# Attention beside a gated feed-forward block on one core: exponent chains of three score pairs on VectorE, merged output groups, and another rule for when paired score tiles are issued

## The chip, the cores and the metric

The kernel runs on one core of one Trainium2 chip. The time is device microseconds of one execution; of several executions the median is given. A separate execution is profiled, and every instruction time below comes from that one.

## What is computed

The input has 2048 rows of 512 bf16 numbers. It is layer-normalized, and the result goes into two branches whose outputs are added to the input: attention with 32 heads of 16 columns, and a gated feed-forward block of width 1792.

```python
def _A_ref(x, wqkv, wo):                     # H = 32, Dh = 16
    qkv = (x @ wqkv).reshape(B, S, 3, H, Dh).transpose(2, 0, 3, 1, 4)
    q, k, v = qkv[0], qkv[1], qkv[2]
    scores = einsum("bhqd,bhkd->bhqk", q, k) * (Dh ** -0.5)
    o = einsum("bhqk,bhkd->bhqd", softmax(scores, axis=-1), v)
    return o.transpose(0, 2, 1, 3).reshape(B, S, D) @ wo

def _B_ref(x, w1, w3, w2):                   # F = 1792
    return (silu(x @ w1) * (x @ w3)) @ w2

return x + _A_ref(layernorm(x), ...) + _B_ref(layernorm(x), ...)
```

The attention needs 32 x 2048 x 2048 exponentials, which is most of the work outside TensorE.

## The kernel before

**Planning.** The program is written by a planner, `_plan_fast`. It steps through time in 0.02 us, keeps a modelled free time for each engine (`P.free`), and whenever an engine is free it picks the next operation for it. The outcome is a fixed order of instructions for each engine, with semaphore waits where data or buffers need them. The planner's durations only decide this order; on the chip an instruction starts when its engine reaches it and its semaphores allow it. A second program, `_plan_max`, stands behind a check of the value ranges; it is in the instruction lists but doesn't run with these inputs.

**Units, pairs and PSUM.** Queries are taken in four chunks of 512 and heads in eight groups of four, which makes 32 units. Inside a unit a score pair is two heads by 128 keys by 512 queries: two matmuls into two neighbouring PSUM banks (`score`, the matmuls at L1803), 128x1024 numbers in all. There are 1056 pairs; the last unit is split into two halves of 256 queries. Banks 0 to 5 are three pair buffers (`pbuf`), bank 6 is the tenant of all dense tiles (projections, feed-forward, output), and bank 7 collects the value products of a unit.

**Two ways to an exponent.** A pair goes to ScalarE (`try_a`, `one_a`): one activation with Exp over 1024 columns (L1866), from PSUM into one of 12 `PT` slots. Or it goes to VectorE (`try_d`): the instruction `p1` (L1939) adds a constant to the scaled score, clips it and writes int16, so that the bits read as a bf16 number near the exponential. Then `chain` improves it with four VectorE instructions on SBUF, over all pairs of a slot at once: `m` (L1981) takes mantissa bits, `g` (L1997) gives a second term, `t` (L1988, two inputs) multiplies, and `e` (L2003) keeps the exponent bits in place. The sum of `e`, `t` and `g` stands for the exponential, so a VectorE pair has three operands where a ScalarE pair has one, and the value matmuls (`try_pv`, L2066) take all three. The slots are three `y`, two `m` and two `g` slots in the tile `xd`, each two pairs (2048 columns) wide; `xd` also holds the input at the start. A chain covers two pairs, except near the end.

**The rule of due times.** `open_bufs` lists the pair buffers that are free. `try_d` issues a score for VectorE if `d_due` allows it: VectorE must be free within `D_SOON` = 0.6 us (`D_RIDE` = 1.0 if a score has just been issued, since matmuls on other rows of the array can run beside it), and the previous chain must have come far enough. `hold_d` lets one such score be outstanding at a time. `try_a` issues one or two scores for ScalarE. With one free buffer it may wait, until `A_SOON` = 0.7 us before ScalarE's queue is modelled to run dry, if a second buffer will be free by then (`A_OVER` = 0.1 more); two pairs with different rows of the array are then issued together. In this test a buffer that is in use and whose release isn't planned yet counts as never free.

**Dense tiles and outputs.** K, Q and V tiles are taken from `crit` a fixed number of score rows before they are needed. Feed-forward and output tiles come from the list `bg`, as filler between scores. A feed-forward tile (`tiles_FFN`) is two dense tiles: G, followed by a tanh on ScalarE (L1555) and a product on VectorE (L1559), and Y, whose product (L1569) writes one of the 14 slots of `hT`. An output tile (`tile_OUT`, 128 rows) is made in two parts: part 3 adds up the 14 feed-forward groups and is evicted with the input added into a float32 sum `osum` (L1619); part 4 adds up the 8 attention groups, later, and is evicted with `osum` added (L1630). The next chunk's feed-forward waits until part 3 has read all of `hT` (`HF`). The last chunk uses parts 3 and 2, and part 5 for the last tile.

**The end of a unit.** `unit_end` copies the value products to SBUF (L2086), and DMAs gather and spread the row sums, VectorE takes the reciprocal (L2106), and GpSimd normalizes (L2127). GpSimd works only beside `p1` (`beside_p1`). The last two halves (`last_end`) use TensorE for the row sums and the spreading (L2168, L2187), VectorE for reciprocal and normalization (L2174, L2195), and ScalarE for the very last copy (L2160).

## Time and profile before

| | |
|---|---|
| median of 3 runs | 790.03 us (788.83 to 790.27) |
| the profiled execution | 789.84 us |
| its span, first to last instruction | 788.1 us |
| ScalarE exponents (L1866) | 796, mean 1151 ns |
| VectorE first steps (L1939) | 228, mean 1216 ns |
| granted TensorE clock, mean | 0.997 |

"Span" runs from the first to the last instruction; some 1.7 us lie around it. Busy time is the union of what an engine's instructions last. Two neighbours on ScalarE or VectorE overlap at their edges[...], so the mean of a group is longer than the pace at which the engine takes such instructions; the pace is the distance between two starts in the timeline. A matmul that stands in the page as 32x512 uses a quarter of the array; four of them on different quarters run side by side and are called a group here. A shape such as 128x2048 is partitions by columns.

The granted clock stays at full speed in nearly all slices, and the DMA engines are busy for about a quarter of the time. POOL is busy for 12% of the span.

### The profile page before, as it was taken

To read this page: it belongs to the slowest core of one execution; us is meant where nothing else is said; L and a number is where in the kernel's file an instruction comes from. 1 tells how busy PE (TensorE), PEld (TensorE's weight loads), DVE (VectorE), ACT (ScalarE), POOL (GpSimd) and SP (SyncE) were. 2 spreads that over 40 slices of the span, in tenths; PEclk is the share of its full clock that TensorE was granted. 3 is DMA by queue.
4 is the path that set the end of the run, shared out by engine and by line. 5 is a ranking of instruction groups with operands and counts; after the bars stand their busy time and mean duration, and the time that the engine had idled before them with its cause. 6 is when DMAs were issued, how large, how long until landed. Compare 5 with 4: busy or idle time off the path is not lost.

```text
span 788.1 us, 21640 instructions
## 1 busy us (share of the span) xinstructions
PE 747.1 (95%) x9337; PEld 226.8 (29%) x9337; DVE 764.8 (97%) x1023; ACT 768.5 (98%) x870; POOL 90.7 (12%) x120
## 2 busy tenths in 40 slices
PE   8999999999999999999999999999899999999997
PEld 6422222222222222222222222222222222222234
DVE  8899999999999999999999999999999999999995
ACT  6999999999999999999999999999999999999994
POOL 3200021002020010201102020010201103010000
PEclk9999999999999999999999999999999999999999
DMA  7023122322332222333302234322222332232121
GB/s 215 2 22 115 9 36 30 49 21 40 51 43 22 30 41 38 47 49 45 50 14 34 22 55 56 41 35 38 34 29 23 56 43 39 49 52 16 20 25 33
DMA packets 83441, 32.94 MB, mean 42 GB/s; under 512 B 72072, under 2 KB 79496, under 8 KB 83336
## 3 DMA queue, kind: packets, MB, share of 16 engines
q1 hardware_dynamic: 83336, 31.46, 28.0%
q8 instruction: 75, 1.23, 0.6%
q14 instruction: 30, 0.25, 0.1%
HBM read 22.81 MB, written 2.10 MB: 32 GB/s over the span
## 4 chain that ended last, share of the span: by engine, by line
ACT 82%; PE 11%; DVE 5%; issue 0%; DMA 0%; POOL 0%; DVEq 0%; ACTq 0%
ACT f_PT L1866 78%; PE ps L1332 4%; PE ps L1803 4%; ACT f_th L1555 3%; PE ps L2066 3%; DVE f_xd L1939 1%; DVE f_xd L1988 1%; DVE f_xd L2003 0%; DVE f_xd L1981 0%; DMA f_xd<-in_A_x_dram 0%; DVE f_hT L1569 0%; PE ps L1344 0%; DVE f_t L1559 0%; DVE f_stats L1256 0%; DVE f_xd L1997 0%
## 5 line engine op out<-in xcount | busy, mean ns | idle before, releaser
L1866 ACT ACTIVATE f_PT<-ps 128x1024 bf16<-128x1024 f32 x796 | 744.7, 1151 | 3.4 <-PE ps L1803 3.2
L1803 PE MATMUL ps<-f_QT,f_KT 32*128 32x512 bf16 (+1 forms) x2112 | 313.6, 378 | 23.3 <-ACT f_PT L1866 17.2
L1939 DVE TENSOR_SCALAR f_xd<-ps 128x1024 int16<-128x1024 f32 x228 | 277.2, 1216 | 2.8 <-PE ps L1803 2.5
L2066 PE MATMUL ps<-f_PT,f_Vaug 128*17 128x512 bf16 (+2 forms) x1640 | 205.1, 378 | 1.1 <-DVE f_U L2086 0.5
L2066 PE MATMUL ps<-f_xd,f_Vaug 128*32 128x512 bf16 (+2 forms) x1416 | 181.9, 377 | 4.6 <-DVE f_U L2086 3.1
L1803 PEld LDWEIGHTS ps<-f_QT,f_KT 32*128 32x128 bf16 x2112 | 80.5, 91 | 322.0 <-ACT f_PT L1866 262.1
L1332 PE MATMUL ps<-f_xnT,f_w 128*32 128x512 bf16 x1792 | 143.1, 386 | 3.7 <-DVE f_t L1559 1.6
L1988 DVE TENSOR_TENSOR f_xd<-f_xd 128x2048 bf16<-128x2048 bf16 (+1 forms) x115 | 139.7, 1215 | 0.0
L1471 POOL TENSOR_SCALAR f_QT<-f_QT,f_msk 128x256 bf16<-128x256 bf16 x60 | 55.3, 922 | 270.5 <-DVE f_xd L1997 112.8
L1981 DVE TENSOR_SCALAR f_xd<-f_xd 128x2048 int16<-128x2048 int16 (+1 forms) x115 | 78.1, 679 | 3.9 <-PE ps L2066 3.1
L2003 DVE TENSOR_SCALAR f_xd<-f_xd 128x2048 int16<-128x2048 int16 (+1 forms) x115 | 78.3, 681 | 0.0
L1997 DVE TENSOR_SCALAR f_xd<-f_xd 128x2048 int16<-128x2048 int16 (+1 forms) x115 | 78.2, 680 | 0.0
L1332 PE MATMUL ps<-f_w,f_hT 128*32 128x512 bf16 x896 | 73.2, 383 | 0.2 <-DVE f_xn_sb L1630 0.2
L2127 POOL TENSOR_TENSOR f_onorm<-f_U,f_R 128x256 bf16<-128x256 f32 x30 | 25.4, 854 | 375.6 <-DMA f_R<-f_Rrow 255.0
L2066 PEld LDWEIGHTS ps<-f_PT,f_Vaug 128*32 128x32 bf16 (+1 forms) x1640 | 51.3, 92 | 58.6 <-issue 45.1
L2066 PEld LDWEIGHTS ps<-f_xd,f_Vaug 128*32 128x32 bf16 (+1 forms) x1416 | 46.1, 92 | 49.0 <-issue 28.5
L1332 PEld LDWEIGHTS ps<-f_xnT,f_w 128*32 128x32 bf16 x1792 | 36.6, 95 | 65.2 <-issue 56.5
L1555 ACT ACTIVATE f_th<-ps 128x512 f32<-128x512 f32 x56 | 40.4, 722 | 0.0
L1569 DVE SCALAR_TENSOR_TENSOR f_hT<-f_t,ps 128x512 bf16<-128x512 bf16 x56 | 37.9, 678 | 1.2 <-PE ps L1332 0.8
L1559 DVE SCALAR_TENSOR_TENSOR f_t<-f_th,ps 128x512 bf16<-128x512 f32 x56 | 37.9, 676 | 0.2
L1332 PEld LDWEIGHTS ps<-f_w,f_hT 128*32 128x32 bf16 x896 | 19.1, 95 | 23.1 <-issue 16.4
L1332 PE MATMUL ps<-f_wo,f_onorm 128*32 128x512 bf16 x272 | 22.1, 383 | 0.3 <-DVE f_wkv L1619 0.2
(82 smaller groups left out, 246.1 us busy)
## 6 DMA issues: line engine op xcount, KB each, us to landing
f_w<-in_B_w_dram SPq DMA_DIRECT2D x112, 128.0 KB
f_R<-f_Rrow SPq DMA_DIRECT2D x124, 32.0 KB
f_xr<-in_A_x_dram SPq DMA_DIRECT2D x16, 128.0 KB
f_U<-f_U SPq DMA_DIRECT2D x60, 32.0 KB
f_w<-in_B_w_dram SPq DMA_DIRECT2D x7, 256.0 KB
f_xd<-in_A_x_dram SPq DMA_DIRECT2D x3, 512.0 KB
out_dram<-f_xn_sb SPq DMA_DIRECT2D x12, 128.0 KB
f_xd<-in_A_x_dram SPq DMA_DIRECT2D x2, 256.0 KB
```

Source lines behind the costliest of these rows:

```text
L1332: ins = e.matmul(bank(bk)[32 * i:32 * i + 32, 0:ncols], make_lhsT(i), rhs_ap, start=start, stop=stop, tile_position=(0, 32 * i))
L1471: q = P.op("pool", lambda e: e.tensor_scalar(QT[:, d_, cs], QT[:, s1, cs], msk[:, h:h + 1], None, ALU.mult), reads=[("QT", s1), ("msk", h) ...
L1555: q = P.op("act", lambda e: e.activation(th[:, ss, :], bank(bk), ACTF.Tanh, scale=0.5), reads=[("ps", bk)], writes=[("th", ss)], dur=a_cos ...
L1559: q2 = P.op("dve", lambda e: e.scalar_tensor_tensor(t1[:, ss, :], th[:, ss, :], 1.0, bank(bk), ALU.add, ALU.mult), reads=[("th", ss), ("ps ...
L1803: ins = e.matmul(b, l_, r_, start=True, stop=True, tile_position=(rp, 0))
L1866: q = P.op("act", lambda e: e.activation(PT[:, s_, :], ps[:, b0 * 512:(b0 + 2) * 512], ACTF.Exp, scale=ASC, bias=ABIAS), reads=[("ps", b0) ...
L1939: q = P.op("dve", lambda e: e.tensor_scalar(dsl[:, ys, 1024 * c:1024 * c + 1024], ps[:, b0 * 512:b0 * 512 + 1024], YB, G_LO, ALU.add, ALU. ...
L1981: P.op("dve", lambda e: e.tensor_scalar(dsl[:, NY + m_, 0:n], y, 0x7F, 0x3F00, ALU.bitwise_and, ALU.bitwise_or), reads=YK, writes=[("ds", ...
L1988: q_ = P.op("dve", lambda e: e.tensor_tensor(t_ap.bitcast(BF16), y.bitcast(BF16), t_ap.bitcast(BF16), ALU.mult), reads=YK + [("ds", NY + m ...
L1997: q_ = P.op("dve", lambda e: e.tensor_scalar(g_ap, y, -G_LO, 0.0, ALU.add, ALU.max), reads=YK, writes=[("g", g_, k) for k in range(n // 51 ...
L2003: q_ = P.op("dve", lambda e: e.tensor_scalar(y, y, 0x7F80, None, ALU.bitwise_and), reads=YK, writes=YK, dur=s_cost(n), name="e", lock=True)
L2066: ins = e.matmul(bank(PV)[32 * j:32 * j + (17 if g % 2 == 0 else 32), pc], v_, p_, start=s0, stop=s1, tile_position=(0, 32 * j))
```

## The change

- **Chains of three.** `ND` = 3: slots of `xd` are three pairs (3072 columns) wide, and a chain covers up to three pairs. `NEED` says how many steps of the previous chain must be done before the first, second and third `p1`. Near the end the width of a chain falls with the pairs that are left (`D_ONE`, `D_PER`).
- **Merged output groups.** For the first three chunks, part 0 takes the place of parts 3 and 4: 14 feed-forward and 8 attention groups accumulate in one PSUM group, and one VectorE instruction (L1636 of the changed kernel) evicts it with the input added. It can start when the chunk's attention is normalized, and stands ahead of other `bg` tiles. `hT` becomes a ring of `NH` = 20 slots, and a feed-forward tile waits only if its slot belongs to a chunk whose output isn't done.
- **Due times.** `second` estimates when a buffer in use will be free (`pest`), instead of counting it as never free; `A_OVER` rises to 0.7 and `D_RIDE` to 1.8. `D_TWO` = 1.8 lets VectorE's score be issued earlier when two buffers are free, and `D_OVER` lets it wait for a second buffer when one is. `try_a` doesn't wait while a score has just been issued (`riding`).
- **GpSimd's Q parts** may also run away from `p1` when their unit is near (`soon`).

The planner works out all orders anew, so instructions move on every engine. The diff, with little of its context:

```diff
@@ -1054,9 +1054,12 @@
     NPR = 12
+    NH = 20
     NON = 6
...
     G_LO = 352.0
+    ND = 3
+    NEED = (1, 2, 2)
     NY = 3
@@ -1065,7 +1068,8 @@
     D_LEFT = 10
-    D_ONE = 11
+    D_ONE = 6
+    D_PER = 5
     D_STOP = 4
@@ -1073,8 +1077,10 @@
     D_SOON = 0.6
-    D_RIDE = 1.0
-    A_OVER = 0.1
+    D_RIDE = 1.8
+    D_TWO = 1.8
+    D_OVER = 0.6
+    A_OVER = 0.7
     A_EARLY = 0.1
@@ -1089,9 +1095,9 @@
     with ctx:
-        xd = sb("xd", [128, max(NT * D, (NY + NM + NG_) * 2048)], I16)
+        xd = sb("xd", [128, max(NT * D, (NY + NM + NG_) * 1024 * ND)], I16)
         x_sb = xd[:, 0:NT * D].bitcast(BF16).rearrange("p (t d) -> p t d", d=D)
-        dsl = xd[:, 0:(NY + NM + NG_) * 2048].rearrange("p (s n) -> p s n", n=2048)
+        dsl = xd[:, 0:(NY + NM + NG_) * 1024 * ND].rearrange("p (s n) -> p s n", n=1024 * ND)
         xr = sb("xr", [128, 2, D], BF16)
@@ -1100,7 +1106,7 @@
         xnT = sb("xnT", [128, DC, S], BF16)
-        hT = sb("hT", [128, FC, 512], BF16)
+        hT = sb("hT", [128, NH, 512], BF16)
         wq = sb("wq", [128, DC, D], BF16)
@@ -1149,7 +1155,7 @@
         def xd_keys(slot, a, b):
-            lo, hi = xcov.get(slot, (2048, 0))
+            lo, hi = xcov.get(slot, (1024 * ND, 0))
             if a >= lo and b <= hi:
@@ -1463,7 +1469,10 @@
                     rel(q)
-                    P.post("pool", lambda: part(0), ready=q.end + _LAT, prio=1, cond=beside_p1)
+                    P.post("pool", lambda: part(0), ready=q.end + _LAT, prio=1, cond=soon)
+
+                def soon():
+                    return beside_p1() or st["pos"] > u0 * RPU - 24
 
@@ -1474,7 +1483,7 @@
                     if i < 3:
-                        P.post("pool", lambda: part(i + 1), ready=q.end + _LAT, prio=1, cond=beside_p1)
+                        P.post("pool", lambda: part(i + 1), ready=q.end + _LAT, prio=1, cond=soon)
                 P.post("dve", emit, ready=o.end + _LAT, prio=1)
@@ -1566,9 +1575,9 @@
                 def e1():
-                    q = P.op("dve", lambda e: e.scalar_tensor_tensor(hT[:, fc, :], t1[:, ss, :], 0.5, bank(bk),
+                    q = P.op("dve", lambda e: e.scalar_tensor_tensor(hT[:, idx % NH, :], t1[:, ss, :], 0.5, bank(bk),
                                                                      ALU.mult, ALU.mult),
-                             reads=[("t1", ss), ("ps", bk)], writes=[("hT", fc)], dur=d_cost(512))
+                             reads=[("t1", ss), ("ps", bk)], writes=[("hT", idx % NH)], dur=d_cost(512))
                     done[("hT", sc, fc)] = q.end + _LAT
@@ -1578,7 +1587,7 @@
                     return False
-                if sc > 0 and not all(("HF", (sc - 1) * 4 + i) in done for i in range(4)):
+                if idx >= NH and not all(("OUT", (idx - NH) // FC * 4 + i) in done for i in range(4)):
                     return False
@@ -1600,14 +1609,14 @@
                         lambda: have(key))
-            ffn = [(lambda i, fc=fc: hT[:, fc, ts * 128 + 32 * i:ts * 128 + 32 * i + 32], w2[:, fc, :],
-                    [("hT", fc), ("w2", fc)], None) for fc in range(FC)]
+            ffn = [(lambda i, fc=fc: hT[:, (qc * FC + fc) % NH, ts * 128 + 32 * i:ts * 128 + 32 * i + 32], w2[:, fc, :],
+                    [("hT", (qc * FC + fc) % NH), ("w2", fc)], None) for fc in range(FC)]
             ats = [og(g, (qc * NP + g) % NON, ("ON", qc, g)) for g in range(NP)]
...
             na = NP - 2 if ts < 1 else NP - 1
-            gr = {2: ats[na:] + last_b, 3: ffn + ats[:na] if qc == NQC - 1 else ffn, 4: ats,
+            gr = {0: ffn + ats, 2: ats[na:] + last_b, 3: ffn + ats[:na] if qc == NQC - 1 else ffn,
                   5: ffn + res + ats + last_b}[part]
@@ -1623,7 +1632,10 @@
                         return
-                    if part == 5:
+                    if part == 0:
+                        q = P.op("dve", lambda e: e.tensor_tensor(osb[:, ts, :], bank(bk), xr[:, ts % 2, :], ALU.add),
+                                 reads=[("ps", bk), ("xr", ts % 2)], writes=[("osb", ts), ("xn", ts)], dur=d_cost(512))
+                    elif part == 5:
                         q = P.op("act", lambda e: e.activation(osb[:, ts, :], bank(bk), ACTF.Identity),
@@ -1631,7 +1643,7 @@
                     done[("XE", tg)] = q.end
-                    if part == 4:
+                    if part == 0:
                         P.post("sp", lambda: P.dma(lambda e: e.dma_start(out_v[:, tg, :], osb[:, ts, :]),
@@ -1646,16 +1658,12 @@
                 else:
-                    P.post("dve", e1, ready=o.end + _LAT, prio=1, cond=lambda: part in (2, 4) or ("xr", tg) in done)
+                    P.post("dve", e1, ready=o.end + _LAT, prio=1, cond=lambda: part == 2 or ("xr", tg) in done)
 
             def cond():
-                if part == 4:
-                    return have(("OSUM", tg), ("ON", qc, NP - 1))
                 if part == 2:
...
                 if not have(*[("hT", qc, fc) for fc in range(FC)]):
-                    return False
-                if part == 3 and qc > 0 and ("OUT", (qc - 1) * 4 + ts) not in done:
                     return False
@@ -1667,11 +1675,12 @@
                 P.post("sp", load, ready=P.t, prio=1, cond=lambda: tg < 2 or ("XE", tg - 2) in done)
-            return _T("O%d_%d" % (tg, part), groups, evac, cond=cond, start=None if part in (2, 4) else start)
+            return _T("O%d_%d" % (tg, part), groups, evac, cond=cond, start=None if part == 2 else start)
 
...
         pbuf = [0.0] * 3
+        pest = [0.0] * 3
         pr_free = [0.0] * NPR
@@ -1715,11 +1724,8 @@
                 bg.extend(tiles_FFN(sc, fc))
-            if sc > 0:
-                for ts in range(4):
-                    bg.append(tile_OUT(sc * 4 - 4 + ts, 4))
             for ts in range(4):
-                bg.append(tile_OUT(sc * 4 + ts, 5 if sc == NQC - 1 and ts > 2 else 3))
+                bg.append(tile_OUT(sc * 4 + ts, 0 if sc < NQC - 1 else 5 if ts > 2 else 3))
         for ts in range(3):
@@ -1832,9 +1838,9 @@
             two = len(free) > 1
-            if not two and not st["early"]:
+            if not two and not st["early"] and not riding():
                 due = max(P.t, P.free["act"]) + 0.905 * st["wait_a"] - A_SOON
-                if due > P.t and sorted(pbuf)[1] <= due + A_OVER:
+                if due > P.t and second() <= due + A_OVER:
                     return False
@@ -1842,6 +1848,12 @@
             return True
+
+        def second():
+            return sorted(v if v < 1e8 else w for v, w in zip(pbuf, pest))[1]
+
+        def riding():
+            return P.pem[0] == "row" and P.t < P.pem[2] + 0.1
 
@@ -1852,6 +1864,7 @@
             st["lastA"] = o.end
+            pest[buf] = max(P.free["act"] + 0.915 * st["wait_a"], o.end) + 1.02
             st["wait_a"] += 1
@@ -1886,19 +1899,22 @@
         def d_due():
-            if P.free["dve"] - P.t > (D_RIDE if P.pem[0] == "row" and P.t < P.pem[2] + 0.1 else D_SOON):
+            n = len(open_bufs())
+            if P.free["dve"] - P.t > (D_RIDE if riding() else D_TWO if n > 1 else D_SOON):
+                return False
+            if n == 1 and not riding() and second() <= P.free["dve"] + D_OVER:
                 return False
...
             if sl is None:
-                pv_, need = dprev[0], 1
+                pv_, need = dprev[0], NEED[0]
                 if pv_ is not None and pv_["p1"] < pv_["max"]:
...
             else:
-                if sl["p1"] < 1:
+                if sl["p1"] < sl["n"]:
                     return False
-                pv_, need = sl["prev"], 2
+                pv_, need = sl["prev"], NEED[sl["n"]]
             return pv_ is None or pv_["done"] >= need
@@ -1919,10 +1935,11 @@
                 ndj[u][j0 + i] += 1
+            pest[buf] = max(P.free["dve"], o.end) + 1.25
             pbuf[buf] = 1e9
...
             if sl is None:
-                sl = dcur[0] = {"y": None, "p1": 0, "n": 0, "ch": [], "done": 0, "max": 2 if u < NV - 1 or left[u] > D_ONE else 1}
+                sl = dcur[0] = {"y": None, "p1": 0, "n": 0, "ch": [], "done": 0, "max": max(1, min(ND, (sum(left) - D_ONE) // D_PER))}
             c = sl["n"]
@@ -1948,7 +1965,7 @@
                 dprev[0] = sl
-            need = 1 if c == 0 else 2
+            need = NEED[c]
             P.post("dve", p1, ready=o.end + _LAT, prio=2,
@@ -2218,10 +2235,10 @@
                 tl = None
-                cand = bg[:4 if st["pos"] >= NR else 3] + [x for x in bg[3:] if x.name[0] == "O" and x.name.endswith("_4")]
+                rest = [x for x in bg if not x.name.endswith("_0")]
+                cand = [x for x in bg if x.name.endswith("_0")] + rest[:4 if st["pos"] >= NR else 3]
                 if cand and any(z[0] == 0 for z in crit[:4]):
                     cand = []
-                cand.sort(key=lambda x: not x.name.endswith("_4"))
                 for x in cand:
@@ -2257,8 +2274,6 @@
                             done[("OUT", int(tg_))] = o.end
-                        if pt_ in "35":
-                            done[("HF", int(tg_))] = o.end
                     a.evac(bk, o, rel)
```

## The prediction, made before the changed kernel ran

> **What bounds the kernel now.** I read the busy line first, then the chain of waits, then the waits of ScalarE and VectorE, then the groups with shapes kept apart, and last a stretch of the timeline for the real pace of each instruction.
>
> ```profile
> PE 747.1 (95%) x9337; PEld 226.8 (29%) x9337; DVE 764.8 (97%) x1023; ACT 768.5 (98%) x870; POOL 90.7 (12%) x120
> ACT 82%; PE 11%; DVE 5%; issue 0%; DMA 0%; POOL 0%; DVEq 0%; ACTq 0%
> ```
>
> Two engines are full: ACT 98% and DVE 97%. The chain runs through ACT for 82% of the span. DMA and POOL carry nothing of it.
>
> ```profile
> 230.79 60.50 ACT f_PT L1866 x66
> ACT f_PT L1866 <- PE ps L1803: 3.2, 5, 1.3
> DVE f_xd L1981 <- PE ps L2066: 3.1, 5, 1.0
> DVE f_xd L1939 <- PE ps L1803: 2.5, 6, 0.6
> ```
>
> The first line is a stretch of the chain: 60.50 / 66 = 0.917 us per exponent of a score pair on ACT. The others are waits (total us, times, longest): ACT waits for scores 3.2 us in all, DVE 2.5, and 3.1 for buffers that the value matmuls still read. So the 1056 pairs are split between two saturated engines, and a pair can be moved only by loading the other one.
>
> ```profile
> L1939 DVE TENSOR_SCALAR f_xd<-ps 128x1024 int16<-128x1024 f32 x228 | 277.2, 1216 | 2.8 <-PE ps L1803 2.5
> L1988 DVE TENSOR_TENSOR f_xd<-f_xd 128x2048 bf16<-128x2048 bf16 x113 | 138.3, 1224 | 0.0
> L1981 DVE TENSOR_SCALAR f_xd<-f_xd 128x2048 int16<-128x2048 int16 x113 | 77.3, 684 | 3.5 <-PE ps L2066 2.7
> L1988 DVE TENSOR_TENSOR f_xd<-f_xd 128x1024 bf16<-128x1024 bf16 x2 | 1.4, 684 | 0.0
> L1981 DVE TENSOR_SCALAR f_xd<-f_xd 128x1024 int16<-128x1024 int16 x2 | 0.8, 422 | 0.4 <-PE ps L2066 0.4
> L1619 DVE TENSOR_TENSOR f_wkv<-ps,f_xr 128x512 f32<-128x512 f32 x15 | 10.1, 676 | 0.1
> ```
>
> The mean is what one instruction lasts; neighbours overlap by about 0.08 us, so the pace is start to start:
>
> ```profile
> 303.42 0.68 DVE L1981 TENSOR_SCALAR f_xd<-f_xd 128x2048 int16<-128x2048 int16 x1
> 304.02 1.21 DVE L1939 TENSOR_SCALAR f_xd<-ps 128x1024 int16<-128x1024 f32 x1
> 305.15 0.68 DVE L2003 TENSOR_SCALAR f_xd<-f_xd 128x2048 int16<-128x2048 int16 x1
> 305.75 0.68 DVE L1997 TENSOR_SCALAR f_xd<-f_xd 128x2048 int16<-128x2048 int16 x1
> ```
>
> That is 0.60 for a one-input step on 2048 columns and 1.13 for the first step out of PSUM (p1). In the same way the timeline gives 1.14 for the 2048-column product (316.96 to 318.10), 0.34 and 0.60 for 1024 columns (776.08 to 776.42, 776.76 to 777.36) and 0.60 for a 512-column step such as L1619. PE, at a score burst between dense groups:
>
> ```profile
> 203.04 0.40 PE L1332 MATMUL ps<-f_xnT,f_w 128*32 128x512 bf16 x4
> 203.37 0.39 PE L1803 MATMUL ps<-f_QT,f_KT 32*128 32x512 bf16 x2
> 203.69 0.62 PE L1332 MATMUL ps<-f_xnT,f_w 128*32 128x512 bf16 x8
> ```
>
> 0.33 into the burst and 0.32 out of it, against 0.22 between two dense groups ((0.62 - 0.40) for the second four): a burst takes 0.43 us of PE, whether it holds one pair or two with disjoint rows.
>
> [...] 0.34 to 0.60 us from 1024 to 2048 columns leaves 0.08 us fixed. [...] PE shows 95%, yet ACT waits for it only 3.2 us.
>
> **The change part by part.** The instruction orders of the two programs, compared engine by engine, give the counts; the planner decides the split.
>
> *Chains of three.* There are 234 VectorE pairs instead of 228, and 790 ScalarE exponents instead of 796. The chains are 77 of three pairs, one of two, one of one, instead of 113 of two and two of one. No row shows 3072 columns. I extend the line from 1024 to 2048: one-input 0.60 + 0.26 = 0.86, product 1.14 + 0.54 = 1.68, a chain 3 x 0.86 + 1.68 = 4.26. The bounds: the low end, 4.1, has part of the fixed cost gone; the high end, 4.41, is one and a half chains of two (no saving at all). I take 4.26, because the two measured points leave a positive fixed cost and the operations keep their types and layout. Before: 113 x (3 x 0.60 + 1.14 = 2.94) + 2 x 1.62 = 335.5 us. After: 77 x 4.26 + 2.94 + 1.62 = 332.6 us. So the chains save 2.9, and the six more p1 cost 6 x 1.13 = 6.8. The other ends put the chains at -15 or +9 us.
>
> *Merged output groups.* For the first twelve row tiles, feed-forward and attention part go into one PSUM group with one eviction (L1636) instead of L1619 plus L1630. PE's matmuls are the same in number; DVE loses 12 x 0.60 = 7.2 us. Before, the 14 feed-forward groups and the 8 attention groups were separate tenants of bank 6; now one tile keeps it for 22 groups, 8 x 0.22 = 1.8 us more of PE time, perhaps 4 with score bursts between. Queued behind it are the K and Q tiles; they are called 80 to 100 rows (40 to 50 pairs, at 788/1056 = 0.75 us each some 30 us or more) ahead, so this is hidden. The ring of 20 hT slots lets six feed-forward tiles of the next chunk start before the output tiles are done; in ScalarE's order one, three and six of them do at the three chunk ends, and the last tanh stands at exponent 738 of 790 against 741 of 796, so the dense work ends no earlier in proportion. DMA counts stay the same (16 xr loads, 12 single stores); SP's loads are off the chain. I cost this at nothing beyond the 7.2; if the cover of the Q tile were gone, one missed unit start would cost about as much as the 1.31 us hole at 312.4 us.
>
> *A V eviction* (384 columns) goes from DVE (0.47) to ACT (about 0.38, from the 491 ns row of its 384-column copy less the overlap).
>
> *Rule of due times.* It adds no instruction. Score matmuls still number 2112, but they stand in 681 bursts instead of 745, so PE has 64 x 0.43 = 27 us more room, less 6 value groups x 0.22 = 1.3. PE is not the bound, so this is worth at most the waits on it. Against it: a score for ACT may now be held until 0.7 us before ACT runs dry, and one for DVE issued 1.8 us before DVE is free (before: 0.6 or 1.0). From both sides: a gain of ACT's 3.2 us of waits, or a loss worked out below. I take nothing.
>
> *The end.* After the last score burst (775.96 before) ScalarE's last copy comes 2.73 us later (778.69). Now the last one-pair chain stands behind the normalization of the first half, which waits for its spread matmuls behind that burst: 0.32 + 0.22 to those, 0.69 to the normalization (774.55 to 775.24 now), 0.42 for it, 1.62 for the chain, 0.45 for the last value matmuls: 3.7 us. So the end costs 1.0 more.
>
> *Sum.* ACT: -6 x 0.917 + 0.38 = -5.1. DVE: -2.9 + 6.8 - 7.2 - 0.5 = -3.8. Both engines are full, so the span follows the slower, nearer -3.8, plus 1.0 for the end, less the waits that go. Among these is the hole at 312 us (1.31 on ACT, 0.85 + 0.46 on DVE), where PE was late; with more PE room I count it as gone. Result: -3.8 + 1.0 - 1.3 = -4.1. The profiled execution was 789.84 us (span 788.1 and 1.7 around it), so 785.7. It lies 0.2 below the median of 790.03: I predict 785.8.
>
> **Rivals.**
>
> *Less idle as well.* The rule of due times removes most waits: ACT -5.1 - 3.2 = -8.3, and DVE loses 5.6 of its waits on scores and buffers, -9.4. With the end at +1.0: 782.7, and 781.5 if the end isn't longer. For it: the 27 us of PE room. Against: many of ACT's steps are already back to back.
>
> *No change.* The 3072-column step saves half of what I count (chain at 4.34 us, +6 us on DVE), which eats the gain: 77 x 0.08 = 6.2, so 790 or somewhat above.
>
> *Slower: a PSUM pair held too long by DVE.* A DVE score issued up to 1.2 us earlier keeps one of the three pair buffers while p1 waits behind a 1.68 us product. ACT then lives on two. Its refill takes 0.33 into the burst and 0.43 from score to exponent (the late exponent at 312.41 follows its burst at 311.98), together 0.76, or 0.98 when a dense group has just started, against 0.917 of the other exponent: the margin is -0.06 to +0.15. 234 holds x 0.8 us more = 187 us, about 200 exponents more that depend on it. At 0.05 us each that is 10 us: 796. It decides from about 0.02 us each (the 4.1 us gain). For it: ACT is on the chain, and PE's score bursts wait for ACT's releases in 628 cases. Against: the burst count shows more scores issued together, which needs two free buffers.
>
> **How the numbers follow.** A measurement of this kernel can tell 0.2% (1.6 us) from no change. Chances: forecast 0.53 (own range 783 to 788.4), less idle 0.15 (779 to 783), no change 0.12 (788.4 to 791.6), slower 0.20 (791.6 to 802). Faster 0.53 + 0.15 = 0.68. The range 779.5 to 793.5 leaves out little of the second case and about half of the last.
>
> **What would show it.** Right: the 3072-column rows at about 0.95 and 1.76 us each; p1 count 234; output adds 15 down to 3 plus 12; ACT's chain still over 75%, at 0.91 to 0.92 per exponent. The end: the last copy about 3.7 us after the last score burst. The slower case would show as over 10 us of ACT waiting for L1809 scores, and an ACT pace above 0.93. I am wrong if the 3072-column steps cost more than one and a half times the 2048-column ones, or if a wait of DVE on the value matmuls (larger buffers freed later) grows from 3.1 us to over 7.

## The result, and the profile after

The changed kernel takes 787.35 us (median of 6 runs, 785.95 to 788.45) against 790.04 us for the kernel before in the same series (6 runs): ratio 0.9966, 95% interval 0.9953 to 0.9979. A second series gave 787.39 against 789.19 us, ratio 0.9974 (0.9963 to 0.9984). The predicted time was 785.8 us, 1.6 below the median; the measured time lies inside the range of the forecast. The change is 1.8 to 2.7 us, about half of the 4.2 that were forecast. The profiled execution took 785.95 us with a span of 784.1 us at a mean clock of 0.997: 3.9 us less than the profiled one of before, where 4.1 were worked out. It was the fastest of its six, so the medians show less. Both have a mean clock of 0.997, but not in the same way: the kernel before has one stretch of 3.4 us at half clock in its middle, at 308.5 us, and the changed one has none before 779.84 us, which is behind its last matmul.

The busy line and the chain of waits of the changed kernel:

```profile
PE 735.2 (94%) x9361; PEld 233.0 (30%) x9361; DVE 761.3 (97%) x872; ACT 764.2 (97%) x865; POOL 93.7 (12%) x120
ACT 82%; PE 10%; DVE 6%; issue 1%; DMA 0%; POOL 0%; DVEq 0%; ACTq 0%
```

VectorE is busy 3.5 us less than before (764.8 to 761.3; the sum said 3.8) and ScalarE 4.3 us less (768.5 to 764.2; the sum said 5.1). The idle time in the span is as it was, 22.8 us on VectorE (23.3 before) and 19.9 on ScalarE (19.6). So in this pair of executions the gain is work taken off both full engines; in the idle time, a hole that went and a longer end (both below) cancel.

The groups with shapes kept apart:

```profile
L1879 ACT ACTIVATE f_PT<-ps 128x1024 bf16<-128x1024 f32 x790 | 737.9, 1107 | 2.1 <-PE ps L1809 2.0
L1956 DVE TENSOR_SCALAR f_xd<-ps 128x1024 int16<-128x1024 f32 x234 | 284.6, 1216 | 7.1 <-PE ps L1809 7.0
...
L2005 DVE TENSOR_TENSOR f_xd<-f_xd 128x3072 bf16<-128x3072 bf16 x77 | 135.4, 1758 | 0.0
...
L1998 DVE TENSOR_SCALAR f_xd<-f_xd 128x3072 int16<-128x3072 int16 x77 | 73.7, 957 | 0.9
...
L1636 DVE TENSOR_TENSOR f_xn_sb<-ps,f_xr 128x512 bf16<-128x512 f32 x12 | 8.1, 673 | 0.0
L1628 DVE TENSOR_TENSOR f_wkv<-ps,f_xr 128x512 f32<-128x512 f32 x3 | 2.0, 683 | 0.0
```

The row means of 957 and 1758 ns are what was forecast (0.95 and 1.76). The pace stands in the timeline of the changed kernel, VectorE alone:

```profile
423.36 0.95 DVE L1998 TENSOR_SCALAR f_xd<-f_xd 128x3072 int16<-128x3072 int16 x1
424.22 0.95 DVE L2014 TENSOR_SCALAR f_xd<-f_xd 128x3072 int16<-128x3072 int16 x1
425.09 1.75 DVE L2005 TENSOR_TENSOR f_xd<-f_xd 128x3072 bf16<-128x3072 bf16 x1
426.76 1.22 DVE L1956 TENSOR_SCALAR f_xd<-ps 128x1024 int16<-128x1024 f32 x1
```

From start to start a one-input step takes 0.86 to 0.87 us and the product 1.67, so a chain takes 3 x 0.867 + 1.67 = 4.27 us (4.26 was taken). The waits of the two engines:

```profile
DVE f_xd L1956 <- PE ps L1809: 7.0, 16, 1.0
...
ACT f_U L2177 <- PE ps L2083: 2.5, 1, 2.5
...
ACT f_PT L1879 <- PE ps L1809: 2.0, 4, 0.6
```

ScalarE waits 2.0 us for scores in the whole run (3.2 before), VectorE's first steps 7.0 (2.5 before). VectorE's wait for buffers that the value matmuls read, 3.1 us before, no longer stands among its waits; all idle time ahead of the L1998 row is 0.9 us. The pace of ScalarE's exponents between 40 and 740 us, taken from the starts in the trace, is 0.92 us in both kernels.

### The profile page after: what moved, and what is told of

Read it like the earlier page. It is cut to its first block, busy times and chain, and to the rows that moved or that the text cites. A ratio compares the mean times of both kernels' runs of the same rounds, so it can differ in the third digit from the quotient of the medians.

```text
span 784.1 us, 21514 instructions
## 1 busy us (share of the span) xinstructions
PE 735.2 (94%) x9361; PEld 233.0 (30%) x9361; DVE 761.3 (97%) x872; ACT 764.2 (97%) x865; POOL 93.7 (12%) x120
## 4 chain that ended last, share of the span: by engine, by line
ACT 82%; PE 10%; DVE 6%; issue 1%; DMA 0%; POOL 0%; DVEq 0%; ACTq 0%
ACT f_PT L1879 78%; PE ps L1338 3%; ACT f_th L1564 3%; PE ps L1809 3%; PE ps L2083 2%; DVE f_xd L1956 2%; DVE f_xd L2005 1%; DVE f_xd L1998 1%; DVE f_xd L2014 1%; DVE f_t L1568 0%; DVE f_hT L1578 0%; DMA f_xd<-in_A_x_dram 0%; DVE f_xd L2020 0%; PE ps L1350 0%; DVE f_stats L1262 0%
## 5 line engine op out<-in xcount | busy, mean ns | idle before, releaser
L1809 PE MATMUL ps<-f_QT,f_KT 32*128 32x512 bf16 (+1 forms) x2112 | 292.8, 378 | 29.6 <-ACT f_PT L1879 23.2
L1956 DVE TENSOR_SCALAR f_xd<-ps 128x1024 int16<-128x1024 f32 x234 | 284.6, 1216 | 7.1 <-PE ps L1809 7.0
L2083 PE MATMUL ps<-f_xd,f_Vaug 128*17 128x512 bf16 (+2 forms) x1452 | 196.2, 376 | 2.1 <-DVE f_U L2103 1.2
L1809 PEld LDWEIGHTS ps<-f_QT,f_KT 32*128 32x128 bf16 x2112 | 75.4, 91 | 305.5 <-ACT f_PT L1879 237.5
L1338 PE MATMUL ps<-f_xnT,f_w 128*32 128x512 bf16 x1792 | 137.1, 383 | 2.9 <-DVE f_t L1568 1.5
L2005 DVE TENSOR_TENSOR f_xd<-f_xd 128x3072 bf16<-128x3072 bf16 (+1 forms) x79 | 137.3, 1738 | 0.0
L1998 DVE TENSOR_SCALAR f_xd<-f_xd 128x3072 int16<-128x3072 int16 (+1 forms) x79 | 74.8, 947 | 1.1
L2083 PEld LDWEIGHTS ps<-f_PT,f_Vaug 128*17 128x17 bf16 (+1 forms) x1628 | 54.2, 92 | 69.9 <-issue 37.8
L2014 DVE TENSOR_SCALAR f_xd<-f_xd 128x3072 int16<-128x3072 int16 (+1 forms) x79 | 74.4, 942 | 0.0
L2020 DVE TENSOR_SCALAR f_xd<-f_xd 128x3072 int16<-128x3072 int16 (+1 forms) x79 | 74.2, 939 | 0.0
L2083 PEld LDWEIGHTS ps<-f_xd,f_Vaug 128*32 128x32 bf16 (+1 forms) x1452 | 50.5, 92 | 52.3 <-issue 32.8
```

Source lines behind the costliest of these rows:

```text
L1338: ins = e.matmul(bank(bk)[32 * i:32 * i + 32, 0:ncols], make_lhsT(i), rhs_ap, start=start, stop=stop, tile_position=(0, 32 * i))
L1809: ins = e.matmul(b, l_, r_, start=True, stop=True, tile_position=(rp, 0))
L1956: q = P.op("dve", lambda e: e.tensor_scalar(dsl[:, ys, 1024 * c:1024 * c + 1024], ps[:, b0 * 512:b0 * 512 + 1024], YB, G_LO, ALU.add, ALU. ...
L1998: P.op("dve", lambda e: e.tensor_scalar(dsl[:, NY + m_, 0:n], y, 0x7F, 0x3F00, ALU.bitwise_and, ALU.bitwise_or), reads=YK, writes=[("ds", ...
L2005: q_ = P.op("dve", lambda e: e.tensor_tensor(t_ap.bitcast(BF16), y.bitcast(BF16), t_ap.bitcast(BF16), ALU.mult), reads=YK + [("ds", NY + m ...
L2014: q_ = P.op("dve", lambda e: e.tensor_scalar(g_ap, y, -G_LO, 0.0, ALU.add, ALU.max), reads=YK, writes=[("g", g_, k) for k in range(n // 51 ...
```

## The experiments

Eleven kernels beside the changed one itself were run. The part of the change on GpSimd's Q parts and the estimates `pest` are in all of them except the kernel before_fewer_tiles; that part was not tried alone. In all of them but merged_and_due, chains_and_due and after_again, the range check of the row sums is also made to wait for the VectorE instruction ahead of it. In the expectations, letters name the readings that are set against one another: in the main A takes parts one by one, as the prediction does, B says that TensorE's room and the one bank of the dense tiles tie the parts together, and C concerns the granted clock.

Each execution comes with its mean granted clock. In every kept trace the clock is either full or half (1.00 or 0.50 of full speed), so (1 - mean clock) x 2 x span is the time at half clock. Over all executions of a kernel a straight line through time against this gives an **estimated time at full clock**, which is used below beside the median. By these lines each us at half clock costs from 0.2 us (merged_and_due) to 0.4 (due_with_filler). Part of that time lies behind the last matmul, where none is left to slow (4.3 us in the profiled execution of the changed kernel, 1.7 in that of before). The kernel before, 110 executions beside the experiments: median 789.22, clock 0.998, 788.1 at full clock; the changed one, 14 executions: clock 0.996, 785.6, which is good to some 0.4 us. Where a kernel has five or six executions the estimate can be off by more; that of due_alone leaves 3 us open, since none of its five has less than 17 us at half clock.

### One part at a time

chains_alone is the kernel before with the chains of three, without merged groups and with the old due times:

```diff
+    ND = 3
+    NEED = (1, 2, 2)
...
-                 "max": 2 if u < NV - 1 or left[u] > D_ONE else 1}
+                 "max": max(1, min(ND, (sum(left) - D_ONE) // D_PER))}
```

> Chains of three alone: old rule of due times, output tiles in two parts. Counts: 229 VectorE pairs, 76 chains of three and one of one, 738 score bursts (before: 228, 745). Theory A (the prediction's sum: PE is not the bound, chains only save VectorE time): VectorE +1.1 - 10.1 = -9.0 us, ScalarE -0.9 us, so 789 to 790 us against 790.0. Theory B (a dense tile in bank 6 waits for its eviction behind VectorE steps of up to 1.68 us, so dense work is done later and PE becomes the bound at the end): behind the last score burst stand 344 dense matmuls instead of 44, some 75 groups x 0.22 = 16 us more, so 798 to 806 us, slower, with ScalarE idle at the end.

merged_alone has part 0 and the ring of 20 slots, with chains of two (`ND` = 2) and the old due times:

```diff
+    NH = 20
-            gr = {2: ats[na:] + last_b, 3: ffn + ats[:na] if qc == NQC - 1 else ffn, 4: ats,
+            gr = {0: ffn + ats, 2: ats[na:] + last_b, 3: ffn + ats[:na] if qc == NQC - 1 else ffn,
```

> Merged output groups and the ring of 20 alone: chains of two, old rule of due times. Counts: 229 VectorE pairs, 739 bursts, 12 evictions fewer. VectorE +1.1 + 1.3 - 7.2 = -4.8 us, ScalarE -0.9 us. Theory A: the span follows ScalarE, -0.9, and the end is as late as in the changed kernel (the last chain behind the first half's normalization), +1.4: 790 to 791 us. Theory B: the same, since 44 dense matmuls stand behind the last burst as before; below 788 would say that the merged group itself frees PE or bank 6.

due_alone has only the new due times (`ND` = 2, parts 3 and 4 as before):

```diff
-    D_RIDE = 1.0
-    A_OVER = 0.1
+    D_RIDE = 1.8
+    D_TWO = 1.8
+    D_OVER = 0.6
+    A_OVER = 0.7
...
+            if not two and not st["early"] and not riding():
+                if due > P.t and second() <= due + A_OVER:
```

> New rule of due times alone: chains of two, output tiles in two parts. Counts: 229 VectorE pairs, 662 bursts instead of 745, 24 dense matmuls behind the last burst instead of 44. Theory A: nothing but the waits, 787.5 to 790 us (ScalarE -0.9, VectorE +2.4, less up to 3 us of waits). Theory B: PE gets 83 x 0.43 = 36 us of room, but with chains of two the dense work was done in time already, so no more than A says. The slower rival of the prediction (buffers held longer by VectorE): 795 us or more, ScalarE's pace above 0.93 us per exponent.

| kernel | median us | ratio to before (95%) | clock | estimate at full clock |
|---|---|---|---|---|
| chains_alone | 805.91 | 1.0210 (1.0195 to 1.0224) | 0.995 | 802.8 |
| merged_alone | 789.51 | 1.0007 (0.9998 to 1.0015) | 0.998 | 788.6 |
| due_alone | 795.56 | 1.0077 (1.0064 to 1.0091) | 0.986 | 788.7 |

Against 788.86 us for before in this series, the three single effects are +17.1, +0.7 and +6.7 us: they add up to +24.4, and all three parts together measured -1.8 to -2.7. No part is a gain by itself, and the parts do not add. There are two different ways of losing here. chains_alone loses at nearly full clock, and its time is in the range of its B. due_alone seems to lose mostly in the clock: the estimate leaves it 0.6 us above before, and two kernels below that share its due times, merged_and_due and due_with_filler, come to 789.0 and 787.4 at full clock. Its A and B (at most 790 us) both missed. The time that was named for the slower rival came, but without its sign: the exponents' pace is 0.925 us, not above 0.93. merged_alone ended half a us below its range.

The waits of chains_alone in its profiled execution, and one of before. That execution was the slowest of the five (811.23 us, clock 0.986), with 20.5 us at half clock inside:

```profile
DVE f_xd L1955 <- PE ps L1811: 19.0, 30, 1.8
ACT f_xn_sb L1634 <- PE ps L1336: 17.2, 1, 17.2
```

```profile
ACT f_xn_sb L1627 <- PE ps L1332: 3.4, 1, 3.4
```

The second line is the end of the program, the third the same wait before. ScalarE has finished all its exponents and waits 17.2 us for dense matmuls of the last output tile (3.4 us before). In TensorE's order 344 dense matmuls stand behind the last score burst, against 44 in the kernel before. The dense work is late. Why, one feed-forward tile shows, in the timeline of the same kernel:

```profile
408.12 0.60 PE L1336 MATMUL ps<-f_xnT,f_w 128*32 128x512 bf16 x4
...
409.02 0.83 PE L1336 MATMUL ps<-f_xnT,f_w 128*32 128x512 bf16 x12
...
409.83 1.75 DVE L2004 TENSOR_TENSOR f_xd<-f_xd 128x3072 bf16<-128x3072 bf16 x1
...
410.12 0.85 ACT L1562 ACTIVATE f_th<-ps 128x512 f32<-128x512 f32 x1
...
411.50 0.68 DVE L2102 COPY f_U<-ps 128x512 f32<-128x512 f32 x1
...
412.10 0.68 DVE L1566 SCALAR_TENSOR_TENSOR f_t<-f_th,ps 128x512 bf16<-128x512 f32 x1
...
413.18 0.61 PE L1336 MATMUL ps<-f_xnT,f_wq 128*32 128x512 bf16 x8
```

G's matmuls begin at 408.12 and are issued by 409.85. The tanh starts at 410.12, and VectorE's product, which frees bank 6, starts only at 412.10: it stands behind the three-pair product of 1.67 us and a unit's copy. The next dense tile begins at 413.18. Bank 6 has one tenant at a time, so every such wait delays all dense work behind it. Taken from the starts and ends of each trace, the mean time from the first matmul of G to the end of its product, plus the same for Y, is 6.82 us per tile pair before and 7.30 in chains_alone: (7.30 - 6.82) x 56 = 27 us more for the 56 pairs. G's and Y's own runs of matmuls are 0.1 us longer each, Y's product comes 0.68 instead of 0.47 us after them, and G's 0.1 us later. Without the tiles that a half-clock stretch touches the two means are 6.80 and 7.22.

The loss of due_alone looks different. This is the granted clock in 40 slices, and below it are windows of its trace (stretch, length, then busy time and instructions of PE, weight loads, DVE, ACT and POOL, then granted clock, DMA share and GB/s):

```profile
PEclk9999999999999999999999999999999999999699
```

```profile
730.00:733.00 3.00, 2.35 (x22) 0.67 (x20) 3.00 (x4) 3.00 (x4) 0.00 (x0) 1.00 0.00 0
733.00:736.30 3.30, 2.43 (x18) 0.66 (x14) 3.30 (x6) 3.30 (x5) 0.00 (x0) 0.95 0.00 0
736.30:740.00 3.70, 3.59 (x28) 0.82 (x28) 3.39 (x5) 2.43 (x4) 0.00 (x0) 0.50 0.16 34
740.00:745.00 5.00, 5.00 (x34) 0.96 (x32) 4.12 (x6) 4.85 (x6) 0.00 (x0) 0.50 0.39 21
```

TensorE has little to do for 3.3 us (18 matmuls, busy 2.43 us), and from 736.0 to 749.6 us the clock is at half. ScalarE, full until then, is busy 2.43 of the next 3.70 us. TensorE was not idle ahead of the half clock, only thinly used. The one half-clock stretch in the middle of the trace of before, at 308.5 us, lasts 3.413 us; this one, 13.6 us, is four times as long, and the 27.3 us in chains_fewer_tiles below are eight times. That thin use sets off the half clock is the reading that fits these windows; what triggers it, and what sets its length, was not shown.

### Two parts at a time

The changed kernel with one part undone each time. merged_and_due goes back to chains of two:

```diff
-    ND = 3
+    ND = 2
```

> The changed kernel with chains of two again (merged groups and new due times stay). Counts: 230 VectorE pairs, 115 chains of two, 649 bursts, 36 dense matmuls behind the last burst. Sum of VectorE: +2.3 + 2.6 - 7.2 - 0.5 = -2.8 us, ScalarE -1.8 + 0.4 = -1.4. Theory A (sum of the counts): 787 to 788.5 us. Theory C (the granted clock: with so few bursts PE runs out of work for a few us at a time, the clock falls to half and scores come late, as in the run with the due times alone, whose mean clock was 0.983 to 0.989): mean clock below 0.993 and 790 to 796 us.

chains_and_merged goes back to the old due times:

```diff
-    D_RIDE = 1.8
-    D_TWO = 1.8
-    D_OVER = 0.6
-    A_OVER = 0.7
+    D_RIDE = 1.0
+    A_OVER = 0.1
...
-                if due > P.t and second() <= due + A_OVER:
+                if due > P.t and sorted(pbuf)[1] <= due + A_OVER:
```

> The changed kernel with the old rule of due times. Counts: 229 VectorE pairs, 735 bursts, 252 dense matmuls behind the last burst instead of 44. Theory A (sum of the counts, VectorE -16, ScalarE -0.9): 788 to 789 us. Theory B (dense work falls behind without PE's room): (252 - 44) / 4 x 0.22 = 11 us more at the end, 797 to 804 us, mean clock above 0.993.

chains_and_due goes back to separate output groups (parts 3 and 4, `NH` = 14):

```diff
-    NH = 20
+    NH = FC
-            gr = {0: ffn + ats, 2: ats[na:] + last_b, 3: ffn + ats[:na] if qc == NQC - 1 else ffn,
+            gr = {2: ats[na:] + last_b, 3: ffn + ats[:na] if qc == NQC - 1 else ffn, 4: ats,
```

> The changed kernel with the output tiles in two parts and 14 hT slots again. Counts: 232 VectorE pairs, 677 bursts, 132 dense matmuls behind the last burst. VectorE +4.5 - 5.9 - 0.5 = -1.9 us, ScalarE -3.3. Theory A: 787 to 788.5 us. Theory B: the dense work is behind, up to (132 - 44) / 4 x 0.22 = 4.8 us more at the end: 789 to 793 us; PE is busy, so the mean clock is above 0.993 and theory C expects no loss.

| kernel | median us | ratio to before (95%) | clock | estimate at full clock | bank 6, us x 56 |
|---|---|---|---|---|---|
| chains_alone | 805.91 | 1.0210 | 0.995 | 802.8 | 7.30: 409 |
| chains_and_merged | 802.40 | 1.0163 (1.0143 to 1.0182) | 0.993 | 799.3 | 7.25: 406 |
| chains_and_due | 795.28 | 1.0063 (1.0049 to 1.0077) | 0.992 | 790.8 | 7.01: 393 |
| before | 789.22 | 1 | 0.998 | 788.1 | 6.82: 382 |
| all three (after) | 787.39 | 0.9974 | 0.996 | 785.6 | 6.79: 380 |
| merged_alone | 789.51 | 1.0007 | 0.998 | 788.6 | 6.65: 372 |
| due_alone | 795.56 | 1.0077 | 0.986 | 788.7 | 6.60: 370 |
| merged_and_due | 794.15 | 1.0060 (1.0036 to 1.0083) | 0.985 | 789.0 | 6.44: 361 |

The rows are in the order of the last column. Above the 380 to 382 us of before and after, the time at full clock rises with it. Below, there is nothing to gain from it, and in two of the three rows the clock is lost instead. So the rule of due times is worth 802.4 - 787.4 = 15 us beside the other two parts, 10.6 beside the chains alone, and costs 4.6 to 6.7 where the chains are of two pairs (at full clock: 13.7, 12.0, and about half a us of cost). Merged groups are worth 8 us beside chains and due times (5.2 at full clock), and chains of three 6.8 beside the other two (3.4 at full clock).

How the rule of due times helps the dense stream can be read from the same tile pairs. In the traces of chains_and_merged and after the score bursts fall from 735 to 681, and a pair's time in bank 6 from 7.25 to 6.79 us: 0.29 of these 0.46 us lie in the runs of matmuls of G and Y, which fewer bursts break into, and the rest in the waits for their products. That the runs shorten because of the bursts is the reading that fits; it was not tried apart from the rule.

Where merged groups are undone, part of the loss shows at the end. ScalarE's last wait for dense matmuls is 3.4 us in the changed kernel; in chains_and_due it is:

```profile
ACT f_xn_sb L1636 <- PE ps L1338: 6.8, 1, 6.8
```

Against the expectations: merged_and_due fits C and chains_and_merged fits B. chains_and_due fits none of them: 795.28 us lie above B's range, and at 0.992 the clock was lost where C expected no loss.

### Is it the dense tiles?

chains_fewer_tiles is chains_alone with two of the 14 feed-forward slices left out (hidden columns 1536 to 1791), so 8 of the 56 tile pairs are missing. before_fewer_tiles is the kernel before with the same cut.

```diff
-    FC = F // 128
+    FC = F // 128 - 2
```

> Chains of three alone, with 12 of the 14 hidden slices of the feed-forward block: the last 256 of its 1792 columns are left out, so 8 of 56 feed-forward tile pairs, and the text reads its time only against the runs without this cut. Work taken off: VectorE 8 x 2 x 0.60 = 9.6 us, ScalarE 8 x 0.48 = 3.8 us, PE 8 x 8 + 16 x 2 groups x 0.22 = 21 us; bank 6 is held 8 x 7.3 + 2 = 60 us less. Theory B (bank 6, one dense tile at a time, is the serial resource that chains of three overload): the time falls to what the two exponent engines allow, some 4 to 6 us below the kernel before, 782 to 788 us, more than 18 us below the 805.9 of the same kernel with all tiles. Theory A (VectorE's and ScalarE's work sets the time): by the work taken off them, about 6 us, so 799 to 801 us.

> The kernel before with the same cut as chains_fewer_tiles: it leaves out the last 256 of the 1792 hidden columns of the feed-forward block, which is 8 of 56 tile pairs. That removes from ScalarE 8 x 0.60 us of tanh and from VectorE 16 x 0.60 us of products, 14.4 us in all; spread over both engines it is at most 7.2 us of span. If the bank of the dense tiles held back only the kernel with long chains and the old rule of due times (theory B), this kernel gains no more than those 7 us at full clock: 782 to 785 us at a clock above 0.995, and more, up to 792, in so far as the thinner stream of matmuls lets the clock fall as it did in chains_fewer_tiles (0.979). If the cut is worth about 15 us to any kernel of this kind (theory A), it lands at 773 to 777.

| | all tiles | 8 pairs left out | difference |
|---|---|---|---|
| before: median us (clock) | 789.64 (0.998) | 788.31 (0.980) | -1.3 |
| chains_alone: median us (clock) | 805.91 (0.995) | 790.72 (0.979) | -15.2 |
| before, at full clock | 788.1 | 781.2 | -6.9 |
| chains_alone, at full clock | 802.8 | 783.2 | -19.6 |

The cut takes the same work out of both kernels, and both end at the same clock. It is worth 13.9 us more to the kernel with long chains (12.7 at full clock), and of its 17 us excess 2.4 are left. ScalarE's wait at the end goes too, as the waits of chains_fewer_tiles show:

```profile
DVE f_xd L1955 <- PE ps L1811: 14.4, 23, 2.4
...
ACT f_xn_sb L1634 <- PE ps L1336: 2.8, 1, 2.8
```

17.2 us have become 2.8, while VectorE still waits 14.4 us for scores. So the excess goes with the dense stream that ends late, and not with the waits of VectorE. The cut takes matmuls away as well as bank time, so these runs don't tell apart whether TensorE's share or the bank is the narrower place; a second dense bank was not tried, since this kernel uses its banks 0 to 7 for scores, dense tiles and value products. The first expectation's range for B, 782 to 788, was missed, and so were the more than 18 us that it named (15.2); at full clock both fit (783.2, and 19.6). The second one's fits, with the clock loss that it allowed for. It takes 0.60 us for a tanh where the first takes 0.48, which is the pace in the trace of before (205.69 to 206.17 us); its 7.2 us are then 6.7.

### Can TensorE be kept busy?

Both kernels add matmuls with zero weights into bank 7, wherever the plan leaves TensorE free; they add zeros to the value products. due_with_filler is due_alone with 200 of them, after_with_filler the changed kernel with 296; after_again is the changed kernel once more, in the same series as the latter.

```diff
+                    elif fill():
...
+                for j in range(4):
+                    ins = e.matmul(bank(PV)[32 * j:32 * j + w_, :], zf[:, 0:w_], wo[:, 0, :],
+                                   start=False, stop=False, tile_position=(0, 32 * j))
```

> The run with the new due times alone, with filler on PE: 50 groups of four matmuls with zero weights, added to the value products in bank 7 where PE would have nothing to do and no pair buffer is about to be free. Theory C (that run lost by the clock): the mean clock goes from 0.986 to 0.995 or more and the time from 795.6 to 788 to 791 us, though PE does more. Rival D (VectorE holds pair buffers too long, or ScalarE's scores are issued too late): the filler changes nothing or costs, 794 us or more, whatever the clock.

> The changed kernel with filler on PE: 74 groups of four matmuls with zero weights into bank 7, where PE would have nothing to do and no pair buffer is about to be free. 789 exponents, 235 VectorE pairs. Theory C (the changed kernel loses about 2 us by stretches at half clock): clock 0.997 or more in most executions, a spread under 2 us, 785 to 787 us. Rival (the stretches are rare enough to be covered by other waits): no faster than the changed kernel beside it, within 0.5 us.

> The changed kernel itself, timed beside the others of this call. 786 to 788.5 us, mean clock 0.994 to 0.999.

due_with_filler: 793.55 us (789.62 to 797.65, 15 runs), ratio 1.0039 (1.0024 to 1.0055), clock 0.991 (0.985 to 0.996) against 0.986 for due_alone. The filler gives back part of the clock and some 2 us; the clock and time that C expected were reached by 5 of the 15 executions, and rival D's 794 us or more were not the median either. That the rule's cost lies in the clock is supported, not proved. after_with_filler: 786.67 us, ratio 0.9964 (0.9951 to 0.9976), clock 0.996 like after_again (787.39, 0.9974, 0.9963 to 0.9984), which lies in its range. The intervals overlap, and only 4 of the 9 executions reached the 0.997 that C asked for: this one is inconclusive.

### The end

last_pair_earlier is the changed kernel with VectorE's last pair issued earlier:

```diff
-    D_STOP = 4
+    D_STOP = 8
```

> The changed kernel with VectorE taking no pair among the last eight instead of the last four: 791 exponents, 233 VectorE pairs, no one-pair chain behind the first half's normalization; behind the last burst stand 56 value matmuls instead of 96. The prediction's term for the end (1.0, measured 1.4 us in the profile) says: last ScalarE copy 2.7 to 3.0 us after the last burst instead of 4.2; ScalarE +0.9 us for the pair that comes back, so 786.5 to 787.5 us, about -0.5 against the changed kernel. If the end were no cost, it would be 0.9 us slower than the changed kernel.

The last score burst, the normalization of the first half, the chain behind it, and ScalarE's last copy, in the timeline of the changed kernel, below the first and last of these before:

```profile
775.96 0.39 PE L1803 MATMUL ps<-f_QT,f_KT 32*128 32x256 bf16 x4
...
778.69 0.38 ACT L2160 ACTIVATE f_U<-ps 128x256 f32<-128x256 f32 x1 [1.23 <-PE ps L2066]
```

```profile
770.13 0.39 PE L1809 MATMUL ps<-f_QT,f_KT 32*128 32x256 bf16 x4
...
771.38 0.48 DVE L2212 SCALAR_TENSOR_TENSOR f_onorm<-f_U,f_msk,ps 128x256 bf16<-128x256 f32 x1 [0.90 <-PE ps L2204]
...
772.00 0.43 DVE L1998 TENSOR_SCALAR f_xd<-f_xd 128x1024 int16<-128x1024 int16 x1
...
774.29 0.38 ACT L2177 ACTIVATE f_U<-ps 128x256 f32<-128x256 f32 x1 [2.55 <-PE ps L2083]
```

And the first and last in last_pair_earlier:

```profile
773.32 0.39 PE L1809 MATMUL ps<-f_QT,f_KT 32*128 32x256 bf16 x4
...
775.61 0.38 ACT L2177 ACTIVATE f_U<-ps 128x256 f32<-128x256 f32 x1 [0.80 <-PE ps L2083]
```

In the changed kernel the copy comes 774.29 - 770.13 = 4.16 us after the burst (2.73 before, 3.7 forecast), behind the chain that stands behind the normalization. With the pair earlier it is 2.29, but the last burst itself is 3.2 us later. The time is 787.86 us (ratio 0.9980, 0.9972 to 0.9989), half a us above the changed kernel, where half a us less was expected and 0.9 more if the end cost nothing. The longer end stands in the trace, but that it costs time isn't shown: this remedy moves it to another place. No version that was run is shown to be faster than the changed kernel.

## Why the prediction was right, and where it was not

- **Chains of three.** Right: 4.27 us a chain against 4.26 taken, 77 + 1 + 1 chains, 234 first steps. VectorE's busy time fell by 3.5 against 3.8 in the sum. The rival that needed 4.34 falls with this. What the sum doesn't have is the side effect on the dense tiles (chains_alone: +17 us). And of the 6.8 us that chains of three are worth beside the other two parts, half is the clock by the estimates; without them it falls to 0.985.
- **Merged output groups.** The counts are right (12 evictions at L1636, 3 at L1628), and undoing them costs 8 us. The prediction's reason, 7.2 us of VectorE, is at most part of it: 3.4 us of the loss are a longer wait for dense work at the end, and some comes with the clock (0.992). By themselves they bring nothing (789.51), and beside the chains with the old due times 3.5 us.
- **Rule of due times: the step that failed.** The prediction said "PE is not the bound, so this is worth at most the waits on it" and took nothing. The runs put it at 15 us beside the other two parts. ScalarE's short waits for scores were the wrong measure of TensorE's room: TensorE also feeds the dense tiles, whose lateness shows not in those waits but once, at the end. Long VectorE instructions made the dense stream late (7.30 against 6.82 us a tile pair in chains_alone), and the new rule, with 54 bursts fewer beside the same two parts, let it catch up (from 7.25 to 6.79). In the sum the two errors cancel: the prediction gave the chains no such cost and the rule no such gain. The total of all three parts came near because the kernel forecast was the one in which the two are balanced. The prediction didn't foresee that balance, so in this respect it was luck.
- **The hole at 312 us: right in the profiled execution, wrong in its reason.** It was put down to TensorE being late, and more room was to remove it. Windows of the kernel before show what it was:

```profile
306.00:308.50 2.50, 1.42 (x12) 0.47 (x10) 2.50 (x4) 2.50 (x5) 0.00 (x0) 1.00 0.00 0
308.50:312.00 3.50, 3.50 (x34) 0.93 (x32) 2.51 (x5) 2.59 (x3) 0.00 (x0) 0.51 0.16 33
```

  TensorE was thinly used (1.42 of 2.50 us) and then got half its clock for one stretch of 3.4 us. More room didn't remove such stretches: due_alone and merged_and_due, which have the fewest score bursts (662 and 649), lost the most clock of all kernels with all tiles (0.986 and 0.985). Whether the changed kernel has more of them than the kernel before isn't shown. Its median clock is 0.996 against 0.998, but that counts the time behind the last matmul too, and of its two traces one has a stretch of 3.4 us inside and one has none.

  This is the term of the sum whose size was wrong. At full clock the two kernels differ by 788.1 - 785.6 = 2.5 us, and the sum without the hole gives 3.8 - 1.0 = 2.8. The hole was to bring 1.3 us more. By the estimates the clock costs a median execution 789.2 - 788.1 = 1.1 us before and 787.4 - 785.6 = 1.8 after, so it brings nothing.
- **The end.** Right in place, too small in size: 4.16 - 2.73 = +1.4 us against +1.0.
- **The slower rival, a pair buffer held by VectorE.** Not seen: ScalarE waits 2.0 us for scores (over 10 were named) at an unchanged pace. A slower outcome was close all the same, by another road: every pair of parts is 0.6 to 1.6% slower than before.
- **Less idle as well.** Not seen: the idle time in the span of both engines stayed within 0.5 us. (Of this rival's two ends, 782.7 starts from the median of before and 781.5 from its profiled execution.)

## What to carry to other kernels

Before a change that lengthens single instructions of a full engine, look for who gets buffers back from that engine: here the dense stream through one shared PSUM bank paid for it, at the end of the program, and the few waits of the two full engines on TensorE before the change gave no sign of it. Parts of a tuned plan can't be priced one by one: here each was no gain, each pair a loss, and the three together a gain. And room on TensorE isn't free: where it was thinly used here (busy for 2.43 of 3.3 us in due_alone, 1.42 of 2.5 in before), its clock was at half just after, for 13.6 and 3.4 us.

## What was not expected of the hardware

Half-clock stretches came after windows in which TensorE still ran 18 matmuls in 3.3 us (due_alone) or 12 in 2.5 us (before). Cut into windows of 3.413 us (the length of the stretch in before) in step with the changes of the clock, the 14 traces have 25 windows at full clock between 30 and 775 us that half clock follows. They hold 14 to 26 matmul starts, TensorE is busy for 2.1 to 2.7 us of them, and no gap is longer than 1.1 us; the one of before, from 305.09 us on, has 16 starts, 2.33 us busy and a longest gap of 0.7 us. All six windows with 16 starts or fewer were followed by half clock, and none with 28 or more; half of all windows have 40 or more. In between it went either way. Half-clock stretches inside the program came in multiples of 3.4 us, from 3.413 (before, at 308.5 us) to 27.3 us without a break (chains_fewer_tiles, from 725.3 us), and each us at half clock cost 0.2 to 0.4 us (the lines of merged_and_due and due_with_filler) of a kernel whose chain runs over ScalarE. The spread between executions of one kernel is then mostly one of the clock where it is wide (for due_with_filler, 789.62 to 797.65 us, the line accounts for nine tenths of the variance), so medians of such kernels have to be read with it.
